# Nyström attention and top-1 MoE on one core: shared groups for the inverses of two batches, a guess with stationary values, and a last output in two halves

## The chip, the cores and the metric

The kernel runs on one core of one Trainium2 chip. The metric is the device time of one execution in microseconds (us), as the median of several runs. The engines are named as in the profile: PE is TensorE's matmul stream and PEld its weight loads, DVE is VectorE, ACT is ScalarE, POOL is GpSimd, SP issues the DMAs.

## What is computed

Eight batches of eight heads (576 positions, head size 64) go through attention with 32 landmarks; the rows that come out are routed to one of eight experts each. Cut to what matters:

```python
def _attn_ref(q, k, v):                        # q, k, v: (8, 8, 576, 64)
    q_lm = q.reshape(B, H, 32, 18, D).mean(3);  k_lm = k.reshape(B, H, 32, 18, D).mean(3)
    A, Bm, C = sm(q, k_lm), sm(q_lm, k_lm), sm(q_lm, k)          # scaled softmax
    Z = Bm.T / (norm1(Bm) * norminf(Bm) + 1e-06)
    for _ in range(6):
        Z = 2 * Z - Z @ Bm @ Z
    return A @ Z @ C @ v

def _moe_ref(x, expert_emb, tau, w1, w2):      # x: (4608, 512), 8 experts, hidden size 1024
    logits = normalized(x) @ normalized(expert_emb).T / tau
    for e in experts:
        h = relu(x[mask_e] @ w1[e]);  out[mask_e] = gate[mask_e] * (h @ w2[e])
```

## The kernel before, in words

The program is one straight line of instructions for each engine, written out while the kernel is built. The order is made by a small planner, the class `Weave` (lines 131 to 316). Each step of the work is a generator that asks for engine time with an estimated duration (`V`, `A`, `T`, `G`), waits for flags, and takes and returns buffers. The planner keeps a clock for each engine, picks the ready step of the highest rank (`PRI`, `FIRST`, `rank`), and emits it. `DMA_LAT` is what it adds to the planned end of a load before it takes the data for landed; `MARGIN`, `BMARGIN`, `SLACK` and `EPS` say how close behind its producers a step may be placed. Engines execute in the planned order whatever the real times are. While the flag `moe` is not yet set (the first expert matmul), the planner fills every planned gap of PE with matmuls on a block of ones (`keep_warm`, line 673), whose result nobody reads.

For each batch b the attention steps are:

- `loads` (706): k and q, then v in two halves, all issued by SP. There are two buffers each for k, q and v.
- `sums` (743): the segment sums that give the landmarks, on DVE or on POOL and DVE.
- `inverse` (768): the 32x32 landmark softmax of all eight heads (in two groups g of four heads, on four diagonal blocks of the array), its scale, and the first residual. One group of 8 small matmuls (16 instructions) gives the scores, another the product in `pk`; about 18 small DVE operations lie between.
- `powers` (1056): six steps of squaring the residual and adding to the inverse. Each step is a group of 8 small matmuls (16 instructions, 64 columns; 32 in the last step), a copy and an add.
- `values` and `products` (861, 930), `queries` (968, gated by flag `pb` of `inverse`), `landmarks` (1082), which multiplies inverse and values, then `rows` (1219) and `route` (1244).
- `guess` (1168), for batches 0 and 1 alone: which expert a batch will need, from column sums of v. Ones are the stationary operand and v streams through (10 matmuls of 256 columns); a DVE transpose (1188) and two operations follow, then `choose` (1197). From batch 2 on, `landmarks` calls `choose`.

The expert part of batch b is `weights` (1347, which loads the guessed expert's w1 and w2 after `guess`), `first_scale` and `first_weights` (absolute sums of w1 at line 1374, the scale, the folded weights `ww` at lines 1418 and 1420), `second_weights` (`w2c`), and the bulk of PE's work: `first` (1475, 96 matmuls of 288 columns) and `second` (1506, four row chunks of 24 matmuls of 512 columns and one half chunk). `first(b)` starts when `second(b-1)` is through. `outputs` (1540) scales a finished chunk out of PSUM into one of two `yt` tiles, and SP writes it out. Bulk work has the lowest rank, so PE takes it whenever nothing else is planned.

Of the kernel before, what the change touches and what calls it, by code (L numbers as in the profile page):

```python
# [51 lines left out]
DMA_LAT = 3600.0  # L52
SLACK = 53.2
EPS = 148.0
MARGIN = 549.6
BMARGIN = 400.0
# [11 lines left out]
NSUM = 3  # L68
# [6 lines left out]
BUFS = dict(k=2, q=2, v=2, ek=6, u=3, ec=2, ct=2, ae=3, at=2, st1=4, st2=4, w2=6, ww=2, ht=12, ab=3, yt=2, land=3, wt=3)  # L75

AHEAD = 20000
PRI = {"loads": 897, "sums": 1694, "inverse": 1697, "values": 1597, "queries": 700, "landmarks": 1656, "rows": 500,
       "route": 794, "guess": 844, "weights": 803, "first": 550, "second": 550}
# [41 lines left out]
def head(g, j):  # L121


    return 4 * g + (j ^ g)
# [421 lines left out]
def nystrom_moe(ctx: ExitStack, tc: tile.TileContext, qT, kT, v, emb, w1, w2, out):  # L546
# [77 lines left out]
    con = cst.tile([P, H * E + DM // M * E + 1], F32, name="con")  # L624
# [3 lines left out]
    enB = con[:, H * E:H * E + DM // M * E].rearrange("p (k e) -> p k e", e=E)  # L628
    rtau = con[:, H * E + DM // M * E:]
# [46 lines left out]
    def embeddings():  # L676
# [17 lines left out]
        yield V2(128)  # L694
        vec.tensor_tensor(out=enB, in0=enB, in1=bc(er.unsqueeze(1), [P, DM // M, E]), op=ALU.mult)
# [10 lines left out]
    def loads(b):  # L706
        if b:
            yield "wait", ("loads", b - 1)
        for src, dst, nm in ((kT, kt, "k"), (qT, qt, "q")):
# [6 lines left out]
            for i in range(parts):  # L716
                yield "use", "dma", 3520 / parts
                r = slice(4 // parts * i, 4 // parts * (i + 1))
                sp.dma_start(dst[b][:, r], src[b][:, r])
                for x in range(2 // parts * i, 2 // parts * (i + 1)):  # L720
                    wv.flag((nm, b, x), DMA_LAT)
            wv.flag((nm, b), DMA_LAT)
# [5 lines left out]
    def load_values(b, gg):  # L728
# [10 lines left out]
        wv.flag(("v", b, gg), DMA_LAT)  # L739
# [28 lines left out]
    def inverse(b):  # L768

        yield "wait", ("ks", b)  # L770
        yield "wait", ("qs", b)
        pb, done = yield from early(T(135, cols=128, tiles="heads"), b)
        pbv = pb[:, :, 0:M]
        for g in range(2):
            for j in range(4):
                h = head(g, j)
                r = 64 * (h % 2)
                mm(pbv[32 * j:32 * j + 32, g], sums_of["q", b][r:r + 64, h // 2, :], sums_of["k", b][r:r + 64, h // 2, :])
        wv.flag(("pb", b))
# [4 lines left out]
        yield V(64)  # L784
        bm4 = small("bm4", 2)
        vec.tensor_reduce(bm4, pbv, axis=AX.X, op=ALU.max)
        yield V(64)
        be = small("be", 2, M)
        vec.tensor_tensor(out=be, in0=pbv, in1=bc(bm4.unsqueeze(2), [P, 2, M]), op=ALU.subtract)
        done()  # L790
        yield A(64, 40)
        act.activation(be, be, AF.Exp, scale=SCALE / (SEG * SEG))
        yield V(64)
        bs4 = small("bs4", 2)
        vec.tensor_reduce(bs4, be, axis=AX.X, op=ALU.add)
        yield V(2)
        vec.tensor_scalar(bs4, bs4, 1e-9, None, op0=ALU.add)
        yield V(22)
# [3 lines left out]
        t = x0[b] = wk.tile([P, 2, 2, M], F32, tag="ek", name="ek", bufs=BUFS["ek"])  # L802
        bm = t[:, 0]
        yield V2(64)
        vec.tensor_tensor(out=bm, in0=be, in1=bc(bs4.unsqueeze(2), [P, 2, M]), op=ALU.mult)
        yield VT(64)
        bt = small("bt", 2, M)
        vec.transpose(bt.rearrange("p g m -> p (g m)"), bm.rearrange("p g m -> p (g m)"))

        pk, done = yield from take(T(170, cols=64, tiles="blocks"), 1)  # L810
        pkv = pk[:, 0:64].rearrange("p (g m) -> p g m", m=M)
        for g in range(2):
            for j in range(4):
                r = slice(32 * j, 32 * j + 32)
                mm(pkv[r, g], bt[r, g], bt[r, g])
        nt = nts[b % 2]
        yield V(64)
        vec.tensor_reduce(nt[:, 1, 0:2], bm, axis=AX.X, op=ALU.add, apply_absolute_value=True)
        yield V(64)
        vec.tensor_reduce(nt[:, 0, 0:2], bt, axis=AX.X, op=ALU.add, apply_absolute_value=True)  # L820
# [18 lines left out]
        for g in range(2):  # L839
            yield VP(32)  # L840
            vec.scalar_tensor_tensor(out=t[:, 1, g], in0=pkv[:, g], scalar=rct[:, g:g + 1], in1=ident4,
                                     op0=ALU.mult, op1=ALU.add)
        done()
        wv.flag(("e", b))
        rc = rcs[b] = small("rc", 2, bufs=BUFS["land"])
        yield V(2)
        vec.tensor_scalar(rc, rct[:, 0:2], -1.0, None, op0=ALU.mult)
        wv.flag(("rc", b))
# [207 lines left out]
    def powers(b):  # L1056

        t = x0[b]
        for k in range(6):
            n = 2 if k < 5 else 1  # L1060
            pz, done = yield from take(T(250 if k < 5 else 170, cols=256, tiles="blocks"), 1)
            pzv = pz[:, 0:4 * M].rearrange("p (a g m) -> p a g m", a=2, g=2)
            for g in range(2):
                for j in range(4):
                    r = slice(32 * j, 32 * j + 32)
                    mm(pzv[r, 0:n, g], t[r, 1, g], t[r, 0:n, g])
            yield "get", "ek"
            t2 = wk.tile([P, 2, 2, M], F32, tag="ek", name="ek", bufs=BUFS["ek"])
            if k < 5:
                if (yield "any", (("act", 115), ("dve", 135))) == "act":  # L1070
                    act.copy(t2[:, 1], pzv[:, 1])
                else:
                    vec.tensor_copy(t2[:, 1], pzv[:, 1])
# [575 lines left out]
```

## Time and profile before

| | us |
|---|---|
| runs of the kernel before: lowest, median, highest | 449.02, 449.94, 450.99 |
| the profiled execution: its own time | 449.05 |
| its span, first to last instruction | 447.3 |
| PE busy in the span | 432.4 |
| DVE busy | 328.1 |
| ACT busy | 277.5 |

The busy time of PE contains the filler of `keep_warm`, and matmuls are pipelined, so that the duration of one is longer than the distance to the next. What PE gets done is read from the distance between the starts of successive groups. The profiled execution was 0.9 us below the median of the runs.

### The profile page before, as it was taken

Reading aid. Unit: us, or ns where it says so; the run is one execution under the profiler, and the core shown is the slowest. Engines: PE = TensorE matmul, PEld = TensorE weight load, DVE = VectorE, ACT = ScalarE, POOL = GpSimd, SP = SyncE. Lnnn points to the kernel's source line nnn. Section 1 sums busy time; section 2 is a strip of 40 time slices with the busy share of each in tenths; the row PEclk is TensorE's granted clock in tenths of the full one; section 3 lists DMA queues with packets and bytes.
Section 4 is the critical chain, followed back from the end, with each engine's and each line's share of the span. In section 5 each row is a group of like instructions: output and inputs, shape, how many; then the busy total and the mean of one; then the engine's idle time right before and its main releaser. Section 6 shows DMA issues by size and latency. Waiting matters only on the chain.

```text
span 447.3 us, 13932 instructions
## 1 busy us (share of the span) xinstructions
PE 432.4 (97%) x5628; PEld 245.5 (55%) x5628; DVE 328.1 (73%) x1110; ACT 277.5 (62%) x641; POOL 79.5 (18%) x80
## 2 busy tenths in 40 slices
PE   7999989999999999999999999999999999999994
PEld 3454554456555476455565466555665476457541
DVE  4877989988895689987995769765987669455300
ACT  1359645887655865987478648955597457945210
POOL 3042143422241104303230105001310101010000
PEclk9999999999999999999999999999999999999998
DMA  8687644884239816882595249322550219211011
GB/s 291 247 298 245 273 160 150 287 294 142 107 131 313 285 49 211 293 264 79 195 373 178 101 141 366 104 80 114 179 211 26 101 51 359 84 57 38 13 49 52
DMA packets 29705, 78.21 MB, mean 175 GB/s; under 512 B 2625, under 2 KB 14017, under 8 KB 27841
## 3 DMA queue, kind: packets, MB, share of 16 engines
q1 hardware_dynamic: 29488, 77.15, 48.6%
q8 instruction: 46, 0.75, 0.7%
q14 instruction: 27, 0.21, 0.1%
q10 hardware_dynamic: 144, 0.10, 0.1%
HBM read 61.96 MB, written 15.27 MB: 173 GB/s over the span
## 4 chain that ended last, share of the span: by engine, by line
PE 68%; DVE 21%; DMA 3%; ACT 3%; POOL 2%; issue 1%; SPq 1%; POOLq 0%; ACTq 0%; DVEq 0%
PE ps L583 61%; PE ps L673 5%; DVE ht L1470 4%; DVE w2c L1460 3%; DMA k_t<-kT 2%; POOL half L759 2%; DMA wstage<-w 2%; DVE qsum L762 1%; DVE cm L888 1%; PE ps L935 1%; DVE ksum L762 1%; DVE ww L1420 1%; DVE ae L986 1%; DVE asum L997 1%; ACT w2c L1458 1%
## 5 line engine op out<-in xcount | busy, mean ns | idle before, releaser
L583 PE MATMUL ps<-w2c,ht 128*128 128x512 f16 (+1 forms) x1152 | 208.9, 345 | 1.5 <-DVE w2c L1460 1.3
L583 PEld LDWEIGHTS <-ht 128*128 128x128 f16 (+1 forms) x1152 | 88.5, 102 | 79.4 <-issue 7.4
L583 PE MATMUL ps<-ab,ww 128*128 128x288 f16 x768 | 105.4, 286 | 2.2 <-DVE ht L1470 2.1
L583 PEld LDWEIGHTS <-ww 128*128 128x128 f16 x768 | 72.1, 98 | 34.1 <-issue 12.1
L1468 ACT ACTIVATE ht<-ps 128x288 f16<-128x288 f32 x128 | 51.9, 409 | 37.2 <-PE ps L583 36.5
L1470 DVE SCALAR_TENSOR_TENSOR ht<-ps,ht 128x288 f16<-128x288 f32 x128 | 54.7, 447 | 8.8 <-ACT ht L1468 8.5
L1460 DVE SCALAR_TENSOR_TENSOR w2c<-wstage,wsc,w2c 128x1024 f16<-128x1024 f32 x32 | 41.0, 1281 | 12.4 <-ACT w2c L1458 12.4
L1554 ACT ACTIVATE yt<-ps,gfac 128x512 f32<-128x512 f32 (+1 forms) x29 | 18.4, 635 | 46.5 <-PE ps L583 45.9
L1018 POOL TENSOR_TENSOR ae<-ae,am 128x576 f32<-128x576 f32 x15 | 17.3, 1159 | 101.4 <-DVE am L991 81.2
L1458 ACT ACTIVATE w2c<-wstage,wsc 128x1024 f16<-128x1024 f32 x30 | 34.4, 1149 | 0.6 <-PE ps L583 0.2
L1433 ACT ACTIVATE junk<-wstage 128x1024 bf16<-128x1024 f32 x32 | 33.9, 1059 | 0.3
L1374 ACT ACTIVATE junk<-wstage 128x1024 bf16<-128x1024 f32 x32 | 33.8, 1055 | 0.1
L1257 POOL TENSOR_TENSOR nrm<-ssq,half 128x5 f32<-128x5 f32 x8 | 10.0, 1251 | 124.6 <-ACT junk L1239 124.6
L673 PE MATMUL ps<-ones 128*128 128x512 bf16 (+3 forms) x117 | 28.4, 390 | 2.3 <-POOL ones L608 2.3
L1239 ACT ACTIVATE junk<-ps 128x512 bf16<-128x512 f32 (+1 forms) x40 | 23.9, 597 | 10.5 <-DVE lg L1237 9.8
L759 POOL TENSOR_TENSOR half<-k_t 128x576 f32<-128x576 f32 x14 | 18.2, 1302 | 41.2 <-DMA k_t<-kT 18.5
L1418 ACT ACTIVATE ww<-ps,wsc 128x1024 f16<-128x1024 f32 (+1 forms) x18 | 18.2, 1013 | 9.0 <-PE ps L583 9.0
L1420 DVE SCALAR_TENSOR_TENSOR ww<-ps,wsc,ww 128x1024 f16<-128x1024 f32 (+1 forms) x18 | 20.9, 1160 | 3.3 <-ACT ww L1418 3.0
L759 POOL TENSOR_TENSOR half<-q_t 128x576 f32<-128x576 f32 x13 | 17.3, 1332 | 25.5 <-DVE ksum L762 14.5
L583 PE MATMUL ps<-wgd,ab 64*128 64x136 f16 (+1 forms) x480 | 21.1, 221 | 0.6 <-DVE ht L1470 0.4
L583 PEld LDWEIGHTS <-ab 64*128 64x128 f16 (+1 forms) x480 | 14.4, 96 | 12.0 <-issue 11.3
L583 PEld LDWEIGHTS ps<-ek 32*32 32x32 f32 x768 | 12.3, 104 | 15.4 <-issue 6.0
(203 smaller groups left out, 567.8 us busy)
## 6 DMA issues: line engine op xcount, KB each, us to landing
wstage<-w SPq DMA_DIRECT2D x64, 512.0 KB, 6.9
v<-v SPq DMA_DIRECT2D x16, 512.0 KB, 5.1
out<-yt SPq DMA_DIRECT2D x32, 256.0 KB, 2.6
k_t<-kT SPq DMA_DIRECT2D x7, 1152.0 KB, 6.7
q_t<-qT SPq DMA_DIRECT2D x7, 1152.0 KB, 11.9
abs__135<-ab SPq DMA_DIRECT2D x8, 576.0 KB, 3.1
k_t<-kT SPq DMA_DIRECT2D x2, 576.0 KB, 5.6
q_t<-qT SPq DMA_DIRECT2D x2, 576.0 KB
```

Of the source, the lines that this page charges most:

```text
L583: pe.matmul(o, lhsT, rhs, start=start, stop=stop)
L673: pe.matmul(warmth[:, 0:k * P], ones16, bc(ones16.unsqueeze(1), [P, k, P]), start=True, stop=True)
L759: pool.tensor_tensor(out=half, in0=sv[:, :, 0:9], in1=sv[:, :, 9:18], op=ALU.add)
L1239: act.activation(junk[lo:hi, 0:512].rearrange("p (i g x) -> p i g x", i=2, g=2), pfv[:, :, :, 0:2 * D], AF.Square, accum_out=ssq[lo:hi, cg ...
L1374: act.activation(junk, stage[1, b, q], AF.Square, accum_out=sq[:, q:q + 1])
L1420: vec.scalar_tensor_tensor(out=ww[:, 1], in0=pww, scalar=sc, in1=ww[:, 0], op0=ALU.mult, op1=ALU.subtract)
L1433: act.activation(junk, stage[2, b, q], AF.Abs, accum_out=sq[:, q:q + 1])
L1458: act.activation(w[:, 0], st, AF.Copy, scale=sc)
L1460: vec.scalar_tensor_tensor(out=w[:, 1], in0=st, scalar=sc, in1=w[:, 0], op0=ALU.mult, op1=ALU.subtract)
L1468: act.activation(ht[:, 0, r], ph[:, 0:HS], AF.Relu)
L1470: vec.scalar_tensor_tensor(out=ht[:, 1, r], in0=ph[:, 0:HS], scalar=0.0, in1=ht[:, 0, r], op0=ALU.max, op1=ALU.subtract)
L1554: act.activation(yt[:, 0:n], py[:, 0:n], AF.Copy, scale=fac)
```

## The change

- The inverses and powers of batches 4 and 5 run together, and those of 6 and 7 (`PAIRS`): one group of matmuls and one DVE operation where there were two. The pair starts when the sums of both batches are there. Batches 0 to 3 stay alone. The buffers `ek` hold two batches each and are four in place of six; sums have four buffers (`NSUM`) in place of three.
- `guess`: v is the stationary operand now and one column of ones streams through: 20 weight loads of 128x128 and 20 matmuls of one column in place of 10 matmuls of 256 columns. The sums land on partitions, so the transpose falls away, and the two DVE operations go over 32 in place of 128 elements. The embeddings' table `enB` shrinks alike.
- The last row chunk of the last batch runs as two halves of 256 columns; the first is scaled and written while PE works on the second. The load of the mispredict count into the engines' registers moves ahead of the first half's output.
- The planner takes 2000 ns in place of 3600 for a load of batch 0 (k, q, v and weights); other batches keep 3600 (`DMA_LATE`). Its margins, slack and some ranks differ.

Cut to its core:

```diff
-DMA_LAT = 3600.0
-SLACK = 53.2
-EPS = 148.0
-MARGIN = 549.6
-BMARGIN = 400.0
+DMA_LAT, DMA_LATE = 2000.0, 3600.0
+SLACK = 46.4
+EPS = 181.8
+MARGIN = 436.5
+BMARGIN = 436.5
-NSUM = 3
+NSUM = 4
-BUFS = dict(k=2, q=2, v=2, ek=6, ...)
+PAIRS = (0,), (1,), (2,), (3,), (4, 5), (6, 7)
+BUFS = dict(k=2, q=2, v=2, ek=4, ...)
+def landing(b):
+    return DMA_LATE if b else DMA_LAT
...
-            wv.flag((nm, b), DMA_LAT)
+            wv.flag((nm, b), landing(b))
...
-    def inverse(b):
-        yield "wait", ("ks", b)
-        yield "wait", ("qs", b)
-        pb, done = yield from early(T(135, cols=128, tiles="heads"), b)
+    def inverse(bs):
+        n = len(bs)
+        b0 = bs[0]
+        for b in bs:
+            yield "wait", ("ks", b)
+            yield "wait", ("qs", b)
+        pb, done = yield from early(T(135 if n == 1 else 235, cols=128 * n, tiles="heads"), b0)
...
+            wv.flag(("pb", b))
...
-    def powers(b):
+    def powers(bs, t):
+        n = len(bs)
         for k in range(6):
+            a = 2 if k < 5 else 1
+            pz, done = yield from take(T((250 if k < 5 else 170) + (n - 1) * 112 * a, cols=128 * a * n, tiles="blocks"), 1)
+            for i in range(n):
+                for g in range(2):
+                    for j in range(4):
+                        r = slice(32 * j, 32 * j + 32)
+                        mm(pzv[r, i, 0:a, g], t[r, i, 1, g], t[r, i, 0:a, g])
...
-        ps_, done = yield from take(T(790, cols=1024, tiles="columns"), 1)
-                mm(ps_[32 * j:32 * j + 32, 256 * gg:256 * gg + 256], ones16[:, 0:M], lead[:, c],
-                   start=(c < 4), stop=(c > 0))
-        yield VT(512)
-        vec.transpose(tr.rearrange("p k r -> p (k r)"), ps_)
-        yield V2(128)
-        vec.tensor_tensor(out=pr, in0=bc(tr[:, :, 0:1], [P, DM // M, E]), in1=enB, op=ALU.mult)
+        ps_, done = yield from take(T(1120, cols=2600), 1)
+        for k in range(4):
+            for c in range(5):
+                mm(ps_[:, k:k + 1], lead[:, c, x:x + P], ones16[:, 0:1], start=(c == 0), stop=(c == 4))
+        yield V(32)
+        vec.tensor_tensor(out=pr, in0=bc(ps_[:, 0:4].unsqueeze(2), [P, 4, E]), in1=enB, op=ALU.mult)
...
+            parts = 2 if (b, c) == (B - 1, order[-1]) else 1
+            n = DM // parts
+            for f, x0 in [(f, n * i) for i in range(parts) for f in range(8)]:
...
+                if parts == 2 and f == 7 and x0 == 0:
+                    wv.add(outputs(b, c, py, None, S * b + o, slice(0, n)), boost=EVICT)
...
-            sp.dma_start(out[t0:t0 + P], yt)
+            sp.dma_start(out[t0:t0 + P, cols], yt[:, 0:n])
```

## Rows read from the trace of the kernel before

**Rows 1.** Page, parts 1 and 2: busy us and share; tenths in 40 slices.

```profile
PE 432.4 (97%) x5628; PEld 245.5 (55%) x5628; DVE 328.1 (73%) x1110; ACT 277.5 (62%) x641; POOL 79.5 (18%) x80
...
PE   7999989999999999999999999999999999999994
...
DVE  4877989988895689987995769765987669455300
```

**Rows 2.** Timeline, batch 0's start: start us, duration us, engine, line, operation, count.

```profile
6.36 7.84 PE L673 MATMUL ps<-ones 128*128 128x512 bf16 x36
10.66 2.59 DVE L762 TENSOR_REDUCE qsum<-q_t 128x64 f32<-128x1152 f32 x2
16.44 0.63 PE L583 MATMUL ps<-v,ones 128*32 128x256 bf16 x10
17.16 0.71 DVE L1188 STREAM_TRANSPOSE half<-ps 128x512 f32<-128x512 f32 x1
34.29 0.75 DVE L1008 SCALAR_TENSOR_TENSOR ab<-at,ab 128x576 f16<-128x576 f32 x1
34.40 1.04 ACT L1374 ACTIVATE junk<-wstage 128x1024 bf16<-128x1024 f32 x1
41.42 1.65 PE L583 MATMUL ps<-ab,ww 128*128 128x288 f16 x12
```

**Rows 3.** Busy of PE, PEld, DVE, ACT, POOL by stretch; PEclk, DMA share, GB/s.

```profile
18.00:24.00 6.00, 5.86 (x113) 3.91 (x114) 5.64 (x31) 1.94 (x8) 0.51 (x1) 1.00 0.10 30
24.00:34.00 10.00, 10.00 (x199) 4.89 (x198) 7.75 (x29) 5.30 (x11) 4.18 (x4) 1.00 0.95 347
```

**Rows 4.** Timeline of PE at four places, columns as in rows 2.

```profile
255.43 2.12 PE L583 MATMUL ps<-w2c,ht 128*128 128x512 f16 x9
257.39 0.28 PE L583 MATMUL ps<-gate,dup 128*128 128x1 f32 x2
...
300.84 2.12 PE L583 MATMUL ps<-w2c,ht 128*128 128x512 f16 x9
302.89 0.53 PE L583 MATMUL ps<-wgd,ab 64*128 64x136 f16 x12
...
335.06 0.77 PE L583 MATMUL ps<-v,ct 128*32 128x64 f32 x40
335.75 0.18 PE L583 MATMUL ps<-ws,ones 128*128 128x1 bf16 x1
335.86 0.43 PE L583 MATMUL ps<-ek 32*32 32x64 f32 x16
...
235.32 1.32 PE L583 MATMUL ps<-v,ct 128*32 128x64 f32 x80
236.58 0.43 PE L583 MATMUL ps<-ek 32*32 32x64 f32 x16
```

**Rows 5.** The last output: timeline, and a row of the view of tile yt.

```profile
441.04 0.69 ACT L1554 ACTIVATE yt<-ps,gfac 128x512 f32<-128x512 f32 x1 [4.49 <-PE ps L583]
...
L1551 DVE TENSOR_SCALAR yt<-ps,gfac x11: 474/751/752, 90.4 to 420.2; 128x512 f32<-128x512 f32 x10, 128x256 f32<-128x256 f32 x1
```

**Rows 6.** Timeline where batch 1 enters the expert part.

```profile
102.64 1.28 DVE L1420 SCALAR_TENSOR_TENSOR ww<-ps,wsc,ww 128x1024 f16<-128x1024 f32 x1
104.43 0.79 PE L583 MATMUL ps<-ab,ww 128*128 128x288 f16 x5
```

**Rows 7.** Timeline of batch 4, and batch 5's last sum (the second row).

```profile
168.03 0.27 PE L583 MATMUL ps<-ksum,qsum 64*32 64x32 f32 x16
187.73 0.75 DVE L762 TENSOR_REDUCE qsum<-half 128x64 f32<-128x576 f32 x1
202.25 0.43 PE L583 MATMUL ps<-u,ek 32*32 32x64 f32 x16
246.72 1.28 DVE L1420 SCALAR_TENSOR_TENSOR ww<-ps,wsc,ww 128x1024 f16<-128x1024 f32 x1
263.75 1.64 PE L583 MATMUL ps<-ab,ww 128*128 128x288 f16 x12
```

More of the change, by code (lines that the diff above doesn't have):

```diff
@@ L74 @@
 EARLY = 2
-BUFS = dict(k=2, q=2, v=2, ek=6, u=3, ec=2, ct=2, ae=3, at=2, st1=4, st2=4, w2=6, ww=2, ht=12, ab=3, yt=2, land=3, wt=3)
+PAIRS = (0,), (1,), (2,), (3,), (4, 5), (6, 7)
+BUFS = dict(k=2, q=2, v=2, ek=4, u=3, ec=2, ct=2, ae=3, at=2, st1=4, st2=4, w2=6, ww=2, ht=12, ab=3, yt=2, land=3, wt=3)
 AHEAD = 20000
-PRI = {"loads": 897, "sums": 1694, "inverse": 1697, "values": 1597, "queries": 700, "landmarks": 1656, "rows": 500,
-       "route": 794, "guess": 844, "weights": 803, "first": 550, "second": 550}
+PRI = {"loads": 897, "sums": 1697, "inverse": 1697, "values": 1603, "queries": 703, "landmarks": 1653, "rows": 500,
+       "route": 800, "guess": 844, "weights": 803, "first": 544, "second": 553}
 FIRST = {"loads": 900, "sums": 800, "inverse": 800, "values": 800, "landmarks": 850, "guess": 810, "weights": 800,
@@ L799, in inverse @@
         vec.reciprocal(bs4, bs4)
         yield "get", "ek"
[L802 to L820, printed above, removed]
+        t = residual(n)
@@ new lines, in inverse @@
+        bm = t[:, :, 0]
+        yield V2(64 * n)
+        vec.tensor_tensor(out=bm, in0=be, in1=bc(bs4.unsqueeze(3), [P, n, 2, M]), op=ALU.mult)
+        yield VT(64 * n)
+        bt = small("bt", 2, 2, M)[:, 0:n]
+        for i in range(n):
+            if i:
+                yield VT(64)
+            vec.transpose(bt[:, i].rearrange("p g m -> p (g m)"), bm[:, i].rearrange("p g m -> p (g m)"))
+        pk, done = yield from take(T(170 if n == 1 else 300, cols=64 * n, tiles="blocks"), 1)
+        pkv = pk[:, 0:64 * n].rearrange("p (b g m) -> p b g m", g=2, m=M)
@@ new lines, in inverse @@
+        for i in range(n):
+            for g in range(2):
+                for j in range(4):
+                    r = slice(32 * j, 32 * j + 32)
+                    mm(pkv[r, i, g], bt[r, i, g], bt[r, i, g])
+        nt = nts[b0 % 2]
+        ntv = nt[:, :, 0:2 * n].rearrange("p a (b g) -> p a b g", g=2)
+        yield V(64 * n)
+        vec.tensor_reduce(ntv[:, 1], bm, axis=AX.X, op=ALU.add, apply_absolute_value=True)
+        yield V(64 * n)
+        vec.tensor_reduce(ntv[:, 0], bt, axis=AX.X, op=ALU.add, apply_absolute_value=True)
@@ L837, in inverse, with residual @@
         vec.transpose(rct, ccb)
[L839 to L842, printed above, removed]
-        done()
[L844 to L848, printed above, removed]
+        for i in range(n):
+            for g in range(2):
+                yield VP(32)
+                vec.scalar_tensor_tensor(out=t[:, i, 1, g], in0=pkv[:, i, g], scalar=rct[:, 2 * i + g:2 * i + g + 1],
+                                         in1=ident4, op0=ALU.mult, op1=ALU.add)
+        done()
+        rc = small("rc", 2, 2, bufs=BUFS["land"])[:, 0:n]
+        yield V(2 * n)
+        vec.tensor_scalar(rc, rct[:, 0:2 * n].rearrange("p (b g) -> p b g", g=2), -1.0, None, op0=ALU.mult)
+        for i, b in enumerate(bs):
+            rcs[b] = rc[:, i]
+            wv.flag(("rc", b))
+        wv.add(powers(bs, t), boost=rank("landmarks", b0))
+    def residual(n):
+        return wk.tile([P, 2, 2, 2, M], F32, tag="ek", name="ek", bufs=BUFS["ek"])[:, 0:n]
     def early(work, b):
@@ L1078, in powers @@
             t = t2
-        x0[b] = t
-        wv.flag(("x", b))
+        for i, b in enumerate(bs):
+            x0[b] = t[:, i, 0]
+            wv.flag(("x", b))
+        wv.add(freed("ek", ("w", bs[-1])))
     def landmarks(b):
@@ L1324, in batch @@
             wv.add(guess(b), boost=rank("guess", b))
-        wv.add(inverse(b), boost=rank("inverse", b))
         wv.add(held(b), boost=rank("loads", b))
@@ L1330, in batch @@
         wv.add(landmarks(b), boost=rank("landmarks", b))
-        yield "wait", ("e", b)
-        wv.add(powers(b), boost=rank("landmarks", b))
         for c in range(5):
@@ L1532, in second @@
                                start=st_, stop=sp_)
-                if c == order[-1]:
+                if c == order[-1] and x0 + n == DM:
                     wv.put("ht")
@@ L1582, in nystrom_moe @@
     wv.add(embeddings(), boost=rank("embeddings", 0))
+    for bs in PAIRS:
+        wv.add(inverse(bs), boost=rank("inverse", bs[0]))
     for b in range(B):
```

127 lines of the change are left out of this document (61 added, 66 removed).

## The prediction

> **What bounds the kernel now.** I read the page's busy times and slices first, then PE's timeline group by group, then the start, the end and the neighbourhood of batch 4. PE is busy for 97% of the span and in nearly all of the 40 slices at nine tenths or more, while DVE is loose from the middle on [rows 1]. So after the first expert matmul at 41.42 us [rows 2] the kernel is one unbroken stream of PE, and what shortens the run is PE work that falls away there, one for one. Two other places count. Before 41.42 us PE's busy time is mostly filler: one block of it lasts 7.84 us [rows 2]. There the chain of loads, sums, guess and weights sets the time at which the real stream begins. And after the last matmul one eviction and one write remain [rows 5].
>
> How much PE costs is read from start to start. Nine matmuls of 512 columns take 257.39 - 255.43 = 1.96 us when another whole-array group follows, and 302.89 - 300.84 = 2.05 when a group on parts of the array follows [rows 4]. So a change from the whole array to tiles costs 0.09. A group of 40 small matmul instructions of 64 columns takes 335.75 - 335.06 = 0.69, one of 80 takes 236.58 - 235.32 = 1.26 [rows 4]. That is 0.57 / 40 = 14 ns an instruction and 0.12 fixed for the group. Merging two groups saves the fixed part once, and the change of shape once where the bulk stands ahead of it.
>
> **Part 1, shared groups.** Batches 4 to 7 have 8 groups each (scores, product, six powers), 32 in all; 16 remain. In the timeline of PE from 165 us on, 24 of the 32 follow a whole-array group. The saving is 16 x 0.12 = 1.9, and 16 x 24/32 = 12 changes of shape x 0.09 = 1.1: together 3.0 us, all on PE's stream. If every merged pair saved a change it would be 16 x 0.21 = 3.4. If a group of 32 behaved like two of 16 it would be nothing. The two ends of the range are these; I take 3.0, because the groups of 40 and 80 are the nearest rows. DVE loses about as many small operations, which I cost at nothing: DVE is hidden behind PE in this half of the run.
>
> The change adds a wait: the pair starts when the later batch's sums are there. For the first pair that is 187.73 + 0.75 = 188.5 us, where batch 4 alone began at 168.03 [rows 7]. Behind it stand the powers, the landmarks (202.25), the guess, the load and the folding of the weights, and queries of batch 4, which wait for the scores; q's next load waits for those queries. Now the folded weights are ready at 246.72 + 1.28 = 248.0 and their first matmul comes at 263.75, because the batch before is not through [rows 7]. So 15.7 us are to spare, and I cost the wait at nothing. It costs one for one beyond that.
>
> **Part 2, the guess.** The 10 matmuls of a guess last 0.63 us [rows 2]. No row shows 20 loads of a new block with one column behind each. The nearest is one such pair, 335.86 - 335.75 = 0.11 us with the change of shape in it, so 0.02 without [rows 4]. That gives 20 x 0.02 = 0.4 to 20 x 0.11 = 2.2. A single load can hide behind the work ahead and twenty cannot, so I take the middle, 1.1, as an estimate: +0.5 for batch 1 (-0.2 to +1.6). Batch 0's guess lies among filler and costs nothing but its own delay. The Trainium skill speaks against this part: by "TensorE: Matmul & The Clock Gate", section "LDWEIGHTS (loading the stationary operand)", a load takes its number of columns divided by 1.2 GHz, here 107 ns whatever the depth. By that estimate the guess would cost 2.1 us, batch 1's term would be +1.5, and the total 446.4; the pair of 0.11 agrees if its load was not hidden. DVE loses the transpose of 0.71 us, twice [rows 2], in a stretch where it is the busiest engine after PE.
>
> **Part 3, the start.** Batch 0's loads count as landed 1.6 us sooner in the plan. What can that give? The first inverse stood behind filler until 6.36 + 7.84 = 14.20 us, but its sums were done at 10.66 + 2.59 = 13.25 [rows 2]: 0.9 us. The DMA engines then idle (share 0.10 from 18 to 24 us) until the weights are asked for, and move 347 GB/s from 24 to 34 [rows 3]. The four blocks of w1 are 2.1 MB, about 6 us at that rate, so they are there at some 30 us; the last pass over them starts at 34.40 [rows 2]. The plan, not the data, holds it for over 4 us. A second 1.6 us, for the weights' landing, should therefore be real, and the guess, shorter by the transpose but longer on PE, comes sooner by part of the first. Against that, DVE is busy for 7.75 of those 10 us [rows 3] and for more in the slices after them [rows 1]. The least possible start of the stream is when the first half of the rows is ready, 34.29 + 0.75 = 35.04 [rows 2], 6.4 us before 41.42. If the loads are really later than 2000 ns, engines wait in order behind them and nothing is won, or up to 1 us is lost. I take -2.0: the 1.6 and half of the 0.9, rounded down. Bounds -6.4 and +1.0.
>
> **Part 4, the last output.** The last eviction takes 0.69 us at 512 columns and 0.47 at 256 [rows 5]: 0.22. Its write is 256 KB, and half of that at 347 GB/s [rows 3] is 0.37. The other half goes out under PE's second half. Against this, 24 more matmul starts: 1.96 / 9 = 0.218 us is 4.4 ns over 512 columns at 2.4 GHz, so 24 x 4.4 ns = 0.1. The term is -0.5 (-0.6 to +0.1, if a write's time does not depend on its size). The register load that moves ahead of the output stands in PE's queue between the halves, hidden by queued matmuls; uncovered it would cost its own half microsecond.
>
> **Part 5, the order.** All margins and ranks differ, so the whole order of the stream is new. The trace of before can't show this. PE loses only a few us between 41 and 441 [rows 1], so little can be gained (-1.5) and some lost (+3.0). I take +0.5, because margins against late producers get smaller.
>
> **Sum**, against the profiled execution's own 449.05: -3.0 + 0.5 - 2.0 - 0.5 + 0.5 = -4.5, so 444.55. The median of the runs before is 449.94, 0.9 above that execution, so the forecast is **445.4**.
>
> **Rivals.** A: the start's gain ends at batch 1. Its folded weights are done at 102.64 + 1.28 = 103.92 and used at 104.43 [rows 6], half a microsecond to spare, and DVE is full in this stretch [rows 1]. If the weights of batch 1, whose loads keep 3600, don't come sooner, the earlier stream waits there: 445.4 + 2.0 = 447.4. Against it: DVE has two transposes less, and PE can do attention of later batches meanwhile.
> B, slower than before: the wait of the pair reaches the stream. Batch 4's own chain from scores to landmarks took 202.25 - 168.03 = 34.2 us for some thirty small operations, so it has much room. If the pair's chain keeps that length and begins 20.5 us later, it overruns the 15.7 by 4.8 [rows 7], and wider operations add about half a microsecond: 445.4 + 5.3 = 450.7. It decides from landmarks later than 202.25 + 15.7 = 218 us on.
> C: merging doesn't do what it says, a group of 32 costs two of 16: 445.4 + 3.0 = 448.4. The 40 and 80 speak against it.
>
> **From cases to numbers.** A measurement of this kernel can tell about 0.5% from no change: below 447.7 is faster, above 452.2 slower. Forecast 0.62 (0.57 faster, 0.05 same), own range 441.5 to 447.5; A 0.16 (0.09, 0.07); C 0.10 (0.03 faster, 0.06 same, 0.01 slower); B 0.12 (0.01, 0.06, 0.05). That makes 0.70 faster, 0.24 same, 0.06 slower. The range runs from 441.5, where the start gives most of its bound, to 449.8, which takes in A and C and leaves most of B out.
>
> **What would show it.** Part 1: groups of 32 small matmuls that start about 0.6 us ahead of the next, with 16 groups fewer. Part 2: the guess of batch 1 about 1.1 us on PE, no transpose. Part 3: the first expert matmul at about 39.4 us, and batch 1's still right behind its weights if A holds. Part 4: some 0.5 us less between the last matmul and the end. B: PE idle ahead of batch 4's first expert matmul. The prediction is wrong if PE's waits after 41 us grow by more than 3 us, or if the stream starts no sooner.

## The result and the profile after

The changed kernel takes 444.63 us as the median of three runs (444.18 to 445.5) beside 450.47 for the kernel before, run together with it (449.02 to 451.58). A fourth run of the changed kernel, at a granted clock of 0.753, took 537.43 us and is left out; with it the median is 445.06. The ratio is 0.9871 with a 95% interval of 0.984 to 0.9901: 1.3% faster. The forecast was 445.4, with a range of 441.5 to 449.8.

The profiled execution took 444.18 us, its span is 442.5; before it was 449.05 and 447.3, so 4.87 us less of its own time. The page of after, lines that answer to [rows 1] (busy time; then PE and DVE in 40 slices):

```profile
PE 425.6 (96%) x5654; PEld 244.6 (55%) x5654; DVE 328.1 (74%) x1065; ACT 274.7 (62%) x632; POOL 79.5 (18%) x78
...
PE   7998989999999999999999999999999999999994
...
DVE  5789999998886789876997788775974299746200
```

PE is busy for 6.8 us less. DVE has 45 instructions fewer and the same busy time: the ones that fell away were small, and wider ones took their place. The slices show DVE fuller in the first quarter than before.

To see where the 4.87 us come from, the span is cut at the first expert matmul and at the end of the last matmul. View of busy time by stretch (from:to, length, then busy us and instructions of PE, PEld, DVE, ACT, POOL, PE's granted clock, DMA share, GB/s), before:

```profile
0.00:41.42 41.42, 38.69 (x492) 18.36 (x493) 30.45 (x111) 17.89 (x43) 9.47 (x24) 1.00 0.75 266
41.42:440.95 399.53, 393.68 (x5144) 227.09 (x5136) 297.70 (x999) 258.88 (x597) 70.01 (x57) 1.00 0.47 167
```

and after:

```profile
0.00:39.38 39.38, 35.05 (x484) 16.90 (x484) 29.49 (x109) 17.89 (x42) 7.85 (x22) 1.00 0.75 276
39.38:436.55 397.17, 390.54 (x5178) 227.72 (x5170) 298.17 (x956) 256.78 (x590) 71.65 (x56) 1.00 0.47 169
```

| us, from these rows | before | after | difference | forecast |
|---|---|---|---|---|
| start, to the first expert matmul | 41.42 | 39.38 | -2.0 | -2.0 |
| PE busy in the stream | 393.68 | 390.54 | -3.1 | -2.5 (groups -3.0, guess +0.5) |
| PE idle in the stream (length less busy) | 5.85 | 6.63 | +0.8 | +0.5 |
| last matmul to the end of the span | 6.35 | 5.95 | -0.4 | -0.5 |
| sum | | | -4.8 | -4.5 |

The table says where the time went, not which edit took it there; that is for the experiments.

Three of the steps in rows. The start of after, timeline (start us, duration us, engine, line, operation, count, and in brackets idle time before and what ended it), to lay beside [rows 2]:

```profile
12.97 0.27 PE L590 MATMUL ps<-ksum,qsum 64*32 64x32 f32 x13
15.19 0.64 PE L590 MATMUL ps<-ones,v 128*128 128x1 bf16 x20
18.52 0.15 DVE L1236 CAST gi<-ge 128x1 int32<-128x1 f32 x1
29.61 1.06 ACT L1391 ACTIVATE junk<-wstage 128x1024 bf16<-128x1024 f32 x1
32.37 1.50 DVE L1044 TENSOR_TENSOR ae<-ae,asum 128x576 f32<-128x576 f32 x1
33.86 0.14 DVE L1395 TENSOR_REDUCE wsq<-wsq 128x1 f32<-128x4 f32 x1
34.27 0.16 PE L590 MATMUL ps<-ws,ones 128*128 128x1 bf16 x1 [1.04 <-DVE ws L1063]
39.38 0.30 PE L590 MATMUL ps<-ab,ww 128*128 128x288 f16 x1
```

The last pass over w1 starts 4.8 us sooner than in [rows 2], but the first expert matmul only 2.0. The rows between tell why: the pass ends at 30.67, and the small sum that needs it (L1395) runs on DVE at 33.86, behind attention work that stands ahead of it in DVE's order. PE then waits 1.04 us for it, a wait that before did not have. At this place the transfers were no longer the limit; DVE was.

The shared groups and the guess of batch 1, PE's timeline and one row of its weight loads (PEld):

```profile
283.92 1.46 PE L590 MATMUL ps<-w2c,ht 128*128 128x512 f16 x6
285.31 0.45 PE L590 MATMUL ps<-bt 32*32 32x32 f32 x32
...
298.85 0.65 PE L590 MATMUL ps<-ek 32*32 32x64 f32 x32
299.43 0.82 PE L590 MATMUL ps<-w2c,ht 128*128 128x512 f16 x3
...
45.16 0.67 PEld L590 LDWEIGHTS <-v 128*128 128x128 bf16 x20
45.28 0.64 PE L590 MATMUL ps<-ones,v 128*128 128x1 bf16 x20
45.79 0.90 PE L590 MATMUL ps<-ab,ww 128*128 128x288 f16 x6
```

A power step of one batch in before, to compare:

```profile
294.71 0.42 PE L583 MATMUL ps<-ek 32*32 32x64 f32 x16
295.07 0.60 PE L583 MATMUL ps<-w2c,ht 128*128 128x512 f16 x2
```

A power step of two batches takes 299.43 - 298.85 = 0.58 us from start to start, as forecast; one batch alone took 295.07 - 294.71 = 0.36. So a merged step saves 2 x 0.36 - 0.58 = 0.14, where the forecast had 0.12 and the change of shape beside it. The guess takes 45.79 - 45.28 = 0.51, where 1.1 was forecast.

The last output:

```profile
434.10 2.45 PE L590 MATMUL ps<-w2c,ht 128*128 128x256 f16 x21 [0.63 <-DVE yt L1577]
...
436.65 0.48 DVE L1577 TENSOR_SCALAR yt<-ps,gfac 128x256 f32<-128x256 f32 x1 [2.60 <-PE ps L590]
```

The eviction is down from 0.69 [rows 5] to 0.48, but PE now waits 0.63 us in the middle of the chunk for the eviction of the first half: both halves lie in one PSUM bank. It is a wait that the program sets, for the eviction's semaphore; what the chip would do without it, no run shows. The prediction had not named this wait.

### The profile page after: what moved, and what is told of

Its sections match the earlier page's. It is cut to its first block, busy times and chain, and to the rows that moved or that the text cites. A ratio compares the mean times of both kernels' runs of the same rounds, so it can differ in the third digit from the quotient of the medians.

```text
span 442.5 us, 13931 instructions
## 1 busy us (share of the span) xinstructions
PE 425.6 (96%) x5654; PEld 244.6 (55%) x5654; DVE 328.1 (74%) x1065; ACT 274.7 (62%) x632; POOL 79.5 (18%) x78
## 4 chain that ended last, share of the span: by engine, by line
PE 68%; DVE 26%; issue 2%; ACT 1%; POOL 1%; DVEq 0%; POOLq 0%; ACTq 0%
PE ps L590 62%; DVE ht L1487 5%; PE ps L680 4%; DVE w2c L1477 3%; DVE cm L912 2%; DVE asum L1021 2%; DVE am L1015 1%; PE ps L959 1%; DVE ksum L769 1%; DVE ab L1032 1%; DVE ae L1010 1%; DVE qsum L769 1%; DVE at L1027 1%; DVE ae L1044 1%; DVE asum L880 1%
## 5 line engine op out<-in xcount | busy, mean ns | idle before, releaser
L590 PE MATMUL ps<-w2c,ht 128*128 128x512 f16 (+2 forms) x1176 | 207.1, 341 | 1.6 <-DVE yt L1577 0.6
L590 PEld LDWEIGHTS <-ht 128*128 128x128 f16 (+1 forms) x1176 | 91.3, 102 | 80.4 <-issue 8.3
L1579 ACT ACTIVATE yt<-ps,gfac 128x512 f32<-128x512 f32 (+1 forms) x25 | 15.8, 637 | 38.3 <-PE ps L590 34.4
L1259 ACT ACTIVATE junk<-ps 128x512 bf16<-128x512 f32 (+1 forms) x40 | 23.9, 598 | 21.8 <-DVE lg L1257 14.7
L1475 ACT ACTIVATE w2c<-wstage,wsc 128x1024 f16<-128x1024 f32 x28 | 31.8, 1148 | 1.0 <-PE ps L590 0.6
L1577 DVE TENSOR_SCALAR yt<-ps,gfac 128x512 f32<-128x512 f32 (+1 forms) x16 | 10.9, 682 | 26.0 <-PE ps L590 25.8
L680 PE MATMUL ps<-ones 128*128 128x512 bf16 (+2 forms) x99 | 24.4, 389 | 2.3 <-POOL ones L615 2.3
L766 POOL TENSOR_TENSOR half<-q_t 128x576 f32<-128x576 f32 x13 | 18.3, 1408 | 25.9 <-DVE ksum L769 10.6
L590 PE MATMUL ps<-wgd,ab 64*128 64x136 f16 (+1 forms) x480 | 20.5, 221 | 0.5 <-DVE ab L1032 0.5
```

Of the source, the lines that this page charges most:

```text
L590: pe.matmul(o, lhsT, rhs, start=start, stop=stop)
L680: pe.matmul(warmth[:, 0:k * P], ones16, bc(ones16.unsqueeze(1), [P, k, P]), start=True, stop=True)
L766: pool.tensor_tensor(out=half, in0=sv[:, :, 0:9], in1=sv[:, :, 9:18], op=ALU.add)
L1259: act.activation(junk[lo:hi, 0:512].rearrange("p (i g x) -> p i g x", i=2, g=2), pfv[:, :, :, 0:2 * D], AF.Square, accum_out=ssq[lo:hi, cg ...
L1475: act.activation(w[:, 0], st, AF.Copy, scale=sc)
```

## Experiments

Each is the changed kernel with one edit, unless it says otherwise. Ratios are to the kernel before in the same set of runs; 0.001 is 0.45 us. The sets (after; e1 to e4; e5 to e8; e9 to e12) were not run together, so runs of different sets are compared by ratio. Runs whose intervals overlap are not told apart by time alone, and there the rows decide.

| run | median us | ratio [95%] | start | PE busy in the stream | PE idle in the stream |
|---|---|---|---|---|---|
| before | 450.47 | 1 | 41.42 | 393.68 | 5.85 |
| after | 444.63 | 0.9871 [0.984, 0.9901] | 39.38 | 390.54 | 6.63 |
| e1_again | 444.38 | 0.9878 [0.9838, 0.9919] | 39.98 | 390.59 | 7.01 |
| e2_whole_end | 443.97 | 0.9874 [0.9834, 0.9913] | 40.02 | 390.44 | 6.34 |
| e3_two_banks | 443.50 | 0.9859 [0.9819, 0.9899] | 39.59 | 390.58 | 6.27 |
| e4_single | 447.55 | 0.9944 [0.9921, 0.9968] | 38.98 | 392.65 | 6.91 |
| e5_late | 445.98 | 0.9917 [0.9888, 0.9947] | 40.55 | 390.32 | 6.58 |
| e6_old_guess | 458.73 | 1.0207 [1.0147, 1.0267] | 37.68 | 394.48 | 17.47 |
| e7_old_margins | 451.14 | 1.0018 [0.9988, 1.0049] | 38.25 | 391.80 | 13.29 |
| e8_margin460 | 445.17 | 0.99 [0.9848, 0.9951] | 38.76 | 390.84 | 6.77 |
| e9_in_place | 446.10 | 0.9881 [0.9861, 0.99] | 40.25 | 390.80 | 7.44 |
| e10_old_guess_460 | 457.15 | 1.0152 [1.009, 1.0214] | 38.65 | 396.20 | 13.94 |
| e11_before_pairs | 450.88 | 1.0005 [0.9978, 1.0032] | 41.77 | 391.08 | 8.44 |
| e12_before_guess | 457.04 | 1.012 [1.0097, 1.0143] | 40.70 | 395.48 | 14.04 |

The last three columns are of each run's profiled execution, from the same two rows as above. PE busy is time: where the granted clock is lower, the same matmuls take more of it.

**e1_again**, the yardstick: a slack 1% larger, which gives the very same order of instructions.

```diff
-SLACK = 46.4
+SLACK = 47.0
```

> The changed kernel once more (a slack of 47.0 in place of 46.4 gives the same order of instructions on every engine), as the yardstick for the other runs: 445.1 us within 0.6, span 442.5. If it comes out more than 1 us away, differences of that size between variants mean nothing.

It measures the same. Two executions of one order differ by 0.6 us in the start (39.38 and 39.98) and by 0.4 in PE's idle time. The traces of e2_whole_end, e3_two_banks, e4_single and e8_margin460 have the same order too up to 100 us or further, and their starts run from 38.76 to 40.02. So a difference of less than 1.3 us in the start means nothing by itself.

**e2_whole_end**: the last chunk undivided.

```diff
-            parts = 2 if (b, c) == (B - 1, order[-1]) else 1
+            parts = 1
```

> The last chunk undivided, all else and the order up to it as in the changed kernel. Theory (the halves save 0.22 of eviction and about 0.37 of the write, and pay 0.1 for matmul starts and 0.63 for a wait of the second half on the first half's eviction, seen in the changed kernel's trace): 0.1 us faster than the changed kernel, so the same. Rival (the wait hides behind something else and the halves are worth the forecast 0.5): 0.5 slower, with the time from the last matmul's end to the span's end longer by 0.6 in both cases.

The ratio moves by -0.0004, which the runs can't tell from nothing. The rows agree: undivided, the time after the last matmul is 6.30 us in place of 5.95, 0.35 longer and not the expected 0.6, and the stream is 396.78 in place of 397.17, 0.39 shorter. What the division takes off the eviction and the write it gives back in the stream, by the wait of 0.63 us.

**e3_two_banks**: the division stays, but the second half goes to a PSUM bank of its own.

```diff
+                if f == 0 and x0:
+                    py, done = yield from take(None, 1, "py")
...
-                    wv.add(outputs(b, c, py, None, S * b + o, slice(0, n)), boost=EVICT)
+                    wv.add(outputs(b, c, py, done, S * b + o, slice(0, n)), boost=EVICT)
```

> The two halves of the last chunk in two PSUM banks, so that the second half does not write the bank that the first half's eviction reads; all else as in the changed kernel. Theory (the 0.63 us wait comes from sharing the bank): PE's wait on the eviction is gone and the run is 0.6 us faster than the changed kernel, 444.5. Rival (PE waits there for the register load that stands in its queue): the wait of 0.6 stays and the time is the same.

PE's timeline there:

```profile
431.80 4.64 PE L590 MATMUL ps<-w2c,ht 128*128 128x256 f16 x41
```

The matmuls of both halves run on without a wait, though the register load still stands in PE's queue. So the wait came with the shared bank, and the rival is refuted. The median is the lowest of all kernels, below both before and after; its distance to e1_again (0.0019, 0.9 us) is inside the intervals, its sign is that of the row.

**e4_single**: every batch's inverse alone again.

```diff
-PAIRS = (0,), (1,), (2,), (3,), (4, 5), (6, 7)
+PAIRS = (0,), (1,), (2,), (3,), (4,), (5,), (6,), (7,)
```

> Batches 4 to 7 alone again, each its own groups; the rest of the changed kernel kept, and the order the same up to batch 4. Theory (16 more groups at 0.12 to 0.14 fixed, and three quarters of them at 0.10 for the change of shape): first expert matmul of batch 4 where it was, span longer by 3.0 to 3.5 us, 448.3. Rival (merging saves nothing on PE, or the pair's wait had cost what it saved): within 0.7 of the changed kernel.

The ratio rises by 0.0066, 3.0 us, beside e1_again. The groups of PE by line and form (busy us, mean ns), e4_single:

```profile
L590 PE MATMUL ps<-ek 32*32 32x64 f32 x640 | 17.1, 220 | 0.4 <-DVE ix L1280 0.2
L590 PE MATMUL ps<-bt 32*32 32x32 f32 x128 | 2.6, 196 | 0.6 <-DVE bt L823 0.6
```

and after:

```profile
L590 PE MATMUL ps<-ek 32*32 32x64 f32 x640 | 15.0, 219 | 0.3 <-DVE ix L1280 0.2
L590 PE MATMUL ps<-bt 32*32 32x32 f32 x128 | 2.2, 195 | 0.6 <-DVE bt L823 0.6
```

As many instructions of the same mean duration are busy for less time together when they stand in groups of 32. Rival C (merging saves nothing) is refuted. PE's busy time in the stream differs by 392.65 - 390.54 = 2.1, which is about what 16 merged groups at 0.14 make. The times differ by 3.0. The profiled spans do too (445.5 and 442.5), but 1.0 of that stands behind the last matmul (6.96 us in place of 5.95), where no group is. So 2.1 to 3.0 is as close as the runs come; the forecast was 3.0. Batch 4's first expert matmul came at 260.05, 1.3 later than in after, and not where it was.

**e5_late**: batch 0's loads count 3600 ns again.

```diff
-    return DMA_LATE if b else DMA_LAT
+    return DMA_LATE
```

> The changed kernel, but the planner takes 3600 ns for batch 0's loads too, as before. Theory (the shorter figure lets batch 0's work start sooner, and what it wins stays in the stream of PE): first expert matmul near 41.4 us in place of 39.4, filler of PE some 3 us more, span longer by 1.5 to 2.0, 446.2. Rival (the gain of the start is given back ahead of batch 1's expert part, where batch 1 began its first at 105.7 us against 104.4 before the change): first expert matmul later, but batch 1's at the same place and the time within 0.5 of the changed kernel.

The last pass over w1, and batch 1's first expert matmul, in e5_late:

```profile
32.83 1.04 ACT L1391 ACTIVATE junk<-wstage 128x1024 bf16<-128x1024 f32 x1
...
106.04 0.91 PE L590 MATMUL ps<-ab,ww 128*128 128x288 f16 x6
```

The shorter latency does bring the start forward: the last pass over w1 comes 2.5 to 3.8 us later without it than in the six traces of after's order (29.03 to 30.29), and the first expert matmul at 40.55 is later than any of theirs (38.76 to 40.02), 1.1 us later than their mean, where 2.0 was expected. Whether the kernel keeps that is open. Batch 1's first expert matmul lies inside the six (105.35 to 106.28), batch 2's is at 158.66 beside 158.69 in after, and the profiled span is 443.4 beside 442.5 (after) and 443.5 (e1_again): this is what the rival said. The ratio is 0.0039 higher, 1.8 us, which is what the theory said, but the intervals overlap.

**e6_old_guess**: the guess of before (ten matmuls of 256 columns, the transpose, products over 128), planned as such.

```diff
-        ps_, done = yield from take(T(1120, cols=2600), 1)
+        ps_, done = yield from take(T(790, cols=1024, tiles="columns"), 1)
...
+        yield "get", "half"
+        yield VT(512)
+        vec.transpose(tr.rearrange("p k r -> p (k r)"), ps_)
```

> The changed kernel with the guess of before (ones stationary, v streaming, the transpose and the table of 128 columns). Theory (the 20 loads with one column cost PE about as much as the 10 matmuls did, 0.51 against 0.56, and DVE saves about 1 us a guess): the first weights are asked for 0.5 to 1.5 us later than at 19.7 us, first expert matmul up to 1 us later, time 0 to 1.0 us longer, 444.9. Rival (the forecast's 1.1 us for a guess on PE): 0.5 us shorter.

Neither theory nor rival had this: by the ratios 0.0329, 14.8 us, slower than e1_again, and slower than before by 2.1% (1.5 to 2.7). The start is the earliest of all, but the stream is idle for 17.47 us:

```profile
37.68:449.63 411.95, 394.48 (x5168) 230.29 (x5160) 297.68 (x955) 260.86 (x593) 72.44 (x57) 0.99 0.47 164
```

PE is also busy for 3.9 us more than in after, with ten matmuls fewer. Time at a lower clock is part of it. View by stretch:

```profile
80.00:84.00 4.00, 2.13 (x68) 1.16 (x66) 4.00 (x15) 3.97 (x9) 1.42 (x2) 1.00 0.83 344
84.00:88.00 4.00, 3.42 (x25) 1.37 (x16) 3.97 (x17) 4.00 (x13) 1.65 (x1) 0.58 0.59 179
```

PE, waiting for ACT and DVE, is busy for 2.13 of 4 us, and in the next stretch the granted clock is 0.58 on average. Between 40 and 432 us, in stretches of 4 us, it falls in e6_old_guess, e10_old_guess_460, e11_before_pairs and e12_before_guess, and in no other run of the table. So an order with long waits can cost twice, in idle time and in clock.

About 1 us of DVE work per guess can't cost that directly. Two explanations were left: the old guess is dear because DVE is full where it stands, or the order that the planner makes around it is a bad one. e9_in_place and e10_old_guess_460 tell them apart.

**e7_old_margins**: all parts of the change, with the margins, slack and ranks of before.

```diff
-SLACK = 46.4
-EPS = 181.8
-MARGIN = 436.5
-BMARGIN = 436.5
+SLACK = 53.2
+EPS = 148.0
+MARGIN = 549.6
+BMARGIN = 400.0
...
```

> The changed kernel with the margins, slack and ranks of before. Theory (they move the order and cost or save little in themselves): within 1.5 us of the changed kernel, in either direction. Rival (the margins carry a good part of the gain): 2.5 us or more slower.

The whole gain is gone, 0.0140 or 6.3 us:

```profile
38.25:443.34 405.09, 391.80 (x5174) 228.76 (x5170) 299.61 (x962) 257.44 (x590) 69.36 (x54) 1.00 0.48 166
```

The start is as early and PE has about the same work (391.80); the rest is idle time, 13.29 in place of 6.63, at full clock. As the rival said, the gain hangs on margins, slack and ranks together; which of them counts is not known. They are not poor in themselves: before has the old ones and the least idle time of all, 5.85. No run put the new ones on the kernel before alone.

**e8_margin460**: one margin 5% larger, which reorders the stream from 100 us on.

```diff
-MARGIN = 436.5
+MARGIN = 460.0
```

> The changed kernel with one margin 5% larger (460 in place of 436.5), which gives another order of nearly all of the stream: a yardstick for what a new order alone does. Theory: within 1 us of the changed kernel. If it is 2 us or more away, a difference of this size in the runs that undo one part can't be put down to that part.

0.99, with 6.77 us of idle time. Another order is not in itself a worse one. The yardstick is shorter than its text says: this margin is not in force before the first expert matmul, and the trace shows the order of after on PE, DVE and ACT up to some 100 us. What a new order does in the first quarter, this run can't tell.

**e9_in_place**: the old guess's instructions put into the planned places of the new guess (with a buffer of its own for the transpose, and the larger table of embeddings), so that nothing else in the order moves.

```diff
         yield V(32)
-        vec.tensor_tensor(out=pr, in0=bc(ps_[:, 0:4].unsqueeze(2), [P, 4, E]), in1=enB, op=ALU.mult)
+        vec.transpose(tr.rearrange("p k r -> p (k r)"), ps_)
+        vec.tensor_tensor(out=pr, in0=bc(tr[:, :, 0:1], [P, DM // M, E]), in1=enB, op=ALU.mult)
```

> The guess of before (ten matmuls of 256 columns, the DVE transpose of 128x512, products over 128) stands in the very places of the new guess; nothing else of the order of the changed kernel moves. It adds to the DVE, by the rows of before and after, 0.71 us for the transpose, 0.11 for the products and 0.17 for the sum, about 1.0 us per guess, for batches 0 and 1. Theory (the 14 us of the old guess in the earlier run came from the order that the planner laid out around it): the first guess ends about 1.0 us later, the first expert matmul up to 1.0 us later, batch 1 up to 1.0 more: 445.0 to 446.5 us. Rival (the old guess itself is dear, because the DVE is busy 97% of the stretch up to batch 1): 452 us or more.

```profile
40.25:438.49 398.24, 390.80 (x5168) 227.49 (x5160) 299.79 (x957) 255.96 (x590) 71.73 (x56) 1.00 0.48 169
```

The ratio is that of e1_again within 0.0003; the stream is 0.6 us longer and the start 0.3 later. So in this order the old guess itself costs about 1 us, and the rival's 452 us is refuted. The 14.8 us of e6_old_guess came with the order that was made around the old guess. There the transpose also shares the buffer `half` with the sums of POOL and DVE, which here it doesn't; the two were not taken apart.

**e10_old_guess_460**: e6_old_guess with the margin of e8_margin460.

> The old guess, planned as in the earlier run, but with one margin of the planner 5% larger, which draws another order. Theory (the order is the price, so another draw gives another price): 446 to 453 us, away from the 458.7 of the earlier run. Rival (the old guess costs 14 us in any order): 445.2 + 14, 458 to 460 us.

457.15: the other draw is hardly better, 12.3 us above e1_again by the ratio. The time comes out nearer to the rival's number, yet e9_in_place has ruled out the rival's reason. What this run adds is that the bad order is no single accident of one margin: its order leaves that of e6_old_guess at 43 us on PE. One place of it, DVE and PE in the timeline:

```profile
66.50 0.75 DVE L769 TENSOR_REDUCE ksum<-half 128x64 f32<-128x576 f32 x1 [1.04 <-POOL half L766]
68.64 0.75 DVE L769 TENSOR_REDUCE ksum<-half 128x64 f32<-128x576 f32 x1 [0.93 <-POOL half L766]
69.31 0.21 DVE L1098 COPY ek<-ps 128x64 f32<-128x64 f32 x1
70.78 0.75 DVE L769 TENSOR_REDUCE qsum<-half 128x64 f32<-128x576 f32 x1 [1.25 <-POOL half L766]
71.45 0.21 DVE L1100 TENSOR_TENSOR ek<-ps,ek 128x64 f32<-128x64 f32 x1
71.72 0.65 PE L590 MATMUL ps<-ek 32*32 32x64 f32 x16 [1.91 <-DVE ek L1100]
```

and PE's clock around it, by stretch:

```profile
64.00:68.00 4.00, 3.19 (x39) 1.47 (x38) 2.33 (x5) 0.65 (x4) 2.27 (x3) 1.00 0.86 292
68.00:72.00 4.00, 1.54 (x26) 0.83 (x29) 2.07 (x6) 0.49 (x2) 2.27 (x3) 0.82 0.05 18
72.00:76.00 4.00, 4.00 (x48) 1.91 (x48) 2.96 (x10) 0.96 (x4) 1.56 (x2) 0.50 0.00 0
76.00:80.00 4.00, 4.00 (x87) 1.71 (x75) 3.03 (x11) 0.41 (x2) 1.29 (x2) 0.82 0.26 64
```

DVE takes the sums of a later batch in turns with POOL through one buffer, and stands about 1 us before each. Behind them in DVE's fixed order is the add of a power step, for which PE waits 1.91 us. No engine is busy for more than 2.3 us of the 4 from 68 to 72, PE for 1.54, and in the next 4 us the granted clock is 0.50, on average. It comes back in the stretch from 76 us on, so the waits are paid twice here too. In the profiled executions of after, e1 to e4, e8 and e9, DVE never waits for POOL's half between 40 and 110 us, but up to 100 us these seven have one order and count as one case; in e6, e7, e10, e11 and e12 it does for 2.6 to 5.2 us. But it does for 4.2 in before too, and for 2.5 in e5_late, whose streams are idle for only 5.85 and 6.58 us, so this is one mechanism and not the whole cause: in e6_old_guess PE waits for other things as well, as for `wen` of DVE (1.8 us, at 234.79). No run took the mechanism away by itself.

**e11_before_pairs**: the kernel before with the shared groups alone.

> The kernel before with the shared groups of batches 4 and 5, and 6 and 7 alone; its old guess, old latency, old margins and undivided last output stay. Theory (the groups save 3.2 us of TensorE wherever they stand): TensorE busy about 3 us less, 447.2 us, a ratio of 0.993. Rival (what the groups save turns into waits unless the margins are set for it): TensorE busy about 3 us less, yet 449.5 to 452 us.

```profile
41.77:441.29 399.52, 391.08 (x5144) 225.93 (x5136) 297.95 (x956) 257.64 (x586) 70.89 (x57) 1.00 0.49 167
```

PE is busy for 2.6 us less than before, its idle time grows by 2.6, and the time is that of before. The rival was right: with the margins of before, what the groups save turns into waits. The prediction's premise that PE work which falls away shortens the run one for one did not hold in this order.

**e12_before_guess**: the kernel before with the new guess alone.

> The kernel before with the new guess alone. Theory (the guess takes about 1.0 us off the DVE at either batch, and the start is bound by the late loads that the planner assumes, not by the guess): 449.4 to 450.6 us, at most 1.0 us below before. Rival (the guess carries a large part of the gain): 447 us or less.

```profile
40.70:450.22 409.52, 395.48 (x5154) 227.18 (x5146) 302.50 (x1007) 258.30 (x589) 68.66 (x56) 0.99 0.46 163
```

Neither was right. The start is 0.7 us sooner, and the stream is idle for 14.04 us; the kernel is 1.2% slower than before. An edit that takes work off DVE and adds none to PE makes the kernel slower. The order made around it is the explanation that is left; no run held the order of before with the new guess in it.

## Why the prediction was right, and where not

**Groups, -3.0: right.** The mechanism and the size hold: 0.58 us for a group of 32 beside 0.36 for one of 16, 3.0 us by the times of e4_single, 2.1 and 2.6 by PE's busy time in e4_single and e11_before_pairs. Whether the changes of shape gave their 1.1 is not settled between 2.1 and 3.0.

**The pair's wait, cost nothing: right.** PE's timeline of batch 4 in after, to lay beside [rows 7]:

```profile
174.42 0.36 PE L590 MATMUL ps<-ksum,qsum 64*32 64x32 f32 x32
...
200.96 0.43 PE L590 MATMUL ps<-u,ek 32*32 32x64 f32 x16
...
258.77 0.42 PE L590 MATMUL ps<-ab,ww 128*128 128x288 f16 x2
```

The pair began 6.4 us later than batch 4 alone, not the 20.5 that the forecast allowed: the sums of batch 5 moved forward in the new order. Its landmarks came 1.3 us sooner than before, far from the 218 us at which rival B decides, and PE did not wait ahead of 258.77. Rival B did not come about. But its condition, a start 20.5 us later, was not met, so what such a wait would have cost was not tried.

**Guess, +0.5: the size was wrong.** Twenty loads with one column each took 0.51 us, 25 ns a pair, about what the ten matmuls before took from start to start (0.56; the 0.63 of the prediction is the duration of the group). The middle of 0.4 and 2.2 was a poor choice: the lower bound, 0.02 us a pair, was nearly the truth. The step that failed is that twenty loads can't hide: the trace has all twenty in 0.67 us, overlapping each other and the matmuls. The rule of the Trainium skill that I had weighed ("TensorE: Matmul & The Clock Gate", section "LDWEIGHTS (loading the stationary operand)") would give 2.1 us; the trace does not agree with it as a distance from load to load. Another section of the page of the Trainium skill, "Back-to-back issue gap", states about 25 ns as the floor for matmuls of up to 64 columns, without counting loads; the trace agrees with that figure, with a load ahead of each matmul. The term is 0 or slightly below, not +0.5.

**Start, -2.0: right in sum, and close by luck.** The first expert matmul came at 39.38; 39.4 was forecast. Six executions with this order began between 38.76 and 40.02, so the start could as well have measured -1.4 or -2.7. The prediction's warning about DVE was right: the early transfers ended up waiting for DVE's order at 33.86. The earlier inverse (12.97, where filler ran until 14.20 in [rows 2]), the earlier guess (`gi` at 18.52, before at 21.32) and the earlier last pass over w1 (29.61) are all there. The last pass alone gained 4.8 us, more than the 1.6 and 0.45 of the sum; DVE's order took the rest back.

**Rival A: not in its full size.** Batch 1's first expert matmul came even later than in [rows 6], and right behind its weights (104.11 + 1.28 = 105.39), the sign that the prediction gave for A:

```profile
104.11 1.28 DVE L1437 SCALAR_TENSOR_TENSOR ww<-ps,wsc,ww 128x1024 f16<-128x1024 f32 x1
...
105.65 0.79 PE L590 MATMUL ps<-ab,ww 128*128 128x288 f16 x5
```

View by stretch from the first expert matmul to batch 1's, before and after:

```profile
41.42:104.43 63.01, 60.26 (x971) 34.09 (x964) 56.50 (x193) 41.47 (x104) 22.41 (x18) 1.00 0.67 233
...
39.38:105.65 66.27, 62.38 (x1041) 34.60 (x1034) 64.55 (x207) 47.28 (x113) 24.59 (x18) 1.00 0.65 228
```

PE did 2.1 us more work in that stretch, so the counterargument given with the rival was right: attention of later batches was done meanwhile. But PE was also idle for 3.89 us in place of 2.75. It had the 1.1 back by batch 2 (158.69, before 159.62), where it was idle for 0.20 us in place of 1.32. In the whole stream its idle time grew by 0.8, not by A's 2.0. That the start's gain was kept in full is not shown, as e5_late says. The start of one batch is no measure of the stream.

**Last output, -0.5: right in number, wrong in what it rests on.** The span ends 0.4 us sooner after the last matmul, but the 0.63 us of PE's wait for the shared bank stands against it, as e2_whole_end and e3_two_banks show. The missing term was +0.6; the part's net is about zero. The 0.22 of eviction was also taken between two engines, ACT at 512 columns (0.69) and DVE at 256 (0.47); on DVE alone [rows 5] have 0.75 and 0.47. Together with the guess (0.5 too much) and PE's other idle time it evened out in the sum.

**Order, +0.5, with bounds of -1.5 and +3.0: this is where the prediction was right by less than it looks.** In after, PE's idle time grew by 0.8 us, so the number holds. But the reason given, that margins against late producers got smaller, was no reason for it. The runs show idle times in the stream from 5.85 to 17.47 us for nearly the same work. The same edits with the margins of before give 451.14, and two of the edits alone, on the kernel before, give about 0 (the groups, forecast at -3.0) and +5.4 us by the ratio (the guess). The sum of the parts held because after's order is about as good as before's (6.63 and 5.85 us of idle time). Nothing in the prediction gave a reason for that, so it was luck. The idle time that a poor order added in e6_old_guess, e7_old_margins and e10_old_guess_460, 6.7 to 10.8 us, is larger than all other terms, and in two of them PE's busy time at a lower clock comes on top; the bound of +3.0 was far too narrow, and no row of before could have shown it. Which property of an order makes it poor stays open; one chain of waits was followed at one place (e10_old_guess_460).

## What to carry to other kernels

Where engines run in an order written at build time, cost an edit by its own instructions, and the order by a term of its own with wide bounds. Test an edit twice: with the order held (the instructions swapped in place) and with the order made anew; the ratios of e9_in_place and e6_old_guess, 0.9881 and 1.0207, are 0.0326 apart, 14.7 us; beside the order the two differ in one shared buffer. Read PE's idle time and its granted clock in each trace. When a tile is drained by halves so that the drain overlaps with the work on the second half, give each half its own PSUM bank; here that removed a wait of 0.63 us.

## What was not expected of the hardware

Twenty loads of 128x128 blocks, each with a matmul of one column, run at 25 ns a pair in the middle of other matmuls (0.51 us for the twenty, after, 45.28 to 45.79 us).

PE's granted clock falls in the middle of a kernel that is otherwise bound by PE. In e10_old_guess_460 PE is busy for 1.54 us from 68 to 72 us, and from 72 to 76 the clock is 0.50 (1.2 GHz of 2.4); in e6_old_guess it is 0.58 on average from 84 to 88, after 2.13 us of work from 80 to 84.

The output of the half chunk (64 rows, written as two column halves from 128 partitions, the halves outermost in the access pattern) moves slowly. View by stretch, after:

```profile
417.00:419.00 2.00, 2.00 (x11) 0.94 (x10) 0.00 (x0) 0.00 (x0) 0.00 (x0) 1.00 0.13 39
...
421.00:423.00 2.00, 2.00 (x11) 0.87 (x9) 0.00 (x0) 0.00 (x0) 0.00 (x0) 1.00 0.34 131
```

It keeps a share of 0.13 of the 16 DMA engines at 39 GB/s for the whole 2 us, while a write of 128 full rows, issued at 420.91, is through within the second stretch, at 131 GB/s on average. The Trainium skill, "DMA: Bandwidth & Descriptors", section "Why a DMA increments its semaphore by 16 and not by 1", has a transfer spread over the largest number of engines, up to 16, that divides the outermost dimension of both its sides, here 2 and 128, so two of sixteen; the share of 0.13 agrees with that. Here it cost nothing that the trace shows, because PE works for some 15 us more after it.
